# Up products of a routed two-layer network: token parts side by side in half of the groups

## The chip, the cores and the metric

One Trainium2 chip, of which the program uses one core. That core has a matrix engine (TensorE, PE in the tables), whose weights are loaded by instructions of their own (PEld), a vector engine (VectorE, DVE), a scalar engine (ScalarE, ACT), GpSimd (POOL) and a queue engine (SP) that issues most DMAs. The metric is the device time of one execution in microseconds (us), the median over runs; lower is better.

## The reference, cut to what matters

```
state = alpha[:, :, t, :, None] * state + einsum('bhd,bhe->bhde', k[:, :, t], v[:, :, t])   # for every t
y[:, :, t] = einsum('bhd,bhde->bhe', q[:, :, t], state)
...
skip_score = x @ w_skip                      # x: 3072 tokens of 384 numbers
do_compute = skip_score > 0
...
e_idx = argmax(xc @ w_gate, axis=1)          # 8 experts
for e in range(8):
    mask = e_idx == e
    h = maximum(xc[mask] @ w1[e], 0.0)       # 384 -> 1024
    y[mask] = gate_w[mask, None] * (h @ w2[e])   # 1024 -> 384
out[do_compute] = xc + y
```

A linear attention gives 3072 tokens. Those with a positive skip score go to one expert each, and each expert is two matrix products with a ReLU between. All numbers are float32.

## The kernel before, in words

**Two stages.** The first 114 us are the attention and the routing. The rest, which the change touches, is the method `experts`: eight experts one after the other. An expert works on a fixed number of token places, `USED`, from 240 down to 192. Experts 0 and 1 have fixed numbers; experts 2 to 7 are the other six, sorted on the chip by how many tokens they got, so that the fullest comes first.

**Split products.** Each float32 number is split into a high part in TensorE's own format and a remainder (names end in `h` and `l`). A product is the sum of three: high weight by high token, low weight by high token, high weight by low token. The tokens of an expert, turned so that features lie on partitions, stand in `xx[:, k, part, :]`: for each of three blocks k of 128 features first the high part, then, 256 columns on, the low part.

**One expert.** `up(e, g)`, four groups g, each with two column tiles f of 128: 2 x 3 x 3 = 18 matmuls of `USED` columns into one PSUM bank, each with its own 128x128 weight tile (L806). Then ACT writes the ReLU as high part `hh` (L820) and DVE the remainder `hl` (L821), both straight from the bank. `down(e, j)`, twice, for the two blocks of up to 128 tokens: 8 x 3 = 24 matmuls of 384 columns (L832), then DVE scales and adds (`o`, L835), and POOL scatters the rows to the output (L837). Between the two, `turn(e+1)` transposes the next expert's tokens on TensorE, three blocks by two token blocks (L784), and ACT and DVE split them into `xx` (L786, L787).

**Weights and tokens.** SP loads a weight matrix of an expert in four pieces (L658) into one of two raw buffers in turn: w1, w2, w1, w2 and so on. ACT and DVE split each piece (L672, L675). Two w1 pieces are split ahead of each half of `down`, a w2 piece ahead of each `up`. POOL gathers the token rows of an expert by an indirect DMA for each token block (L640) from a list of row numbers. Each engine's instructions stand in the order in which the program issues them.

**The sorted order.** `order_experts` is a chain of 17 small DVE instructions (L727 to L753). Its first eleven end with `by`, a selector with which two small matmuls reorder the row lists of the experts (`order_rows`, L755, into `by_idx`). The other six give `order_ids`, the experts' numbers (`by_order` in the trace), which SP reads into registers (`load_order`, L770); the addresses of the weight loads of experts 2 to 7 come from them. Before the change the whole chain stands in expert 0 behind `turn(1)`, ahead of the second `down`; `order_rows` and the gather for expert 2 stand inside `up(1, 0)`, and the w1 load of expert 2 behind `down(0, 1)`.

**Banks.** The first `up` of all takes bank 0 of `ps_y`; after that `ps_k`, `ps_s[0]` and `ps_s[1]` take turns. `turn` writes both banks of `ps_y`.

Of the kernel before, what the change touches and what calls it, by code (L numbers as in the profile page):

```python
# [17 lines left out]
ALU = mybir.AluOpType  # L18
# [17 lines left out]
CAP = 256  # L36
USED = (240, 240, 240, 228, 216, 208, 200, 192)
FIXED = 2
VW = 3 * E
NB = CAP // P  # L40
SEG = P + 3
# [23 lines left out]
class Kernel:  # L65
# [612 lines left out]
    def expert_pools(self, st):  # L678
        tc = self.tc
        self.mp = st.enter_context(tc.tile_pool(name="mp", bufs=2))  # L680
        self.wpool["w2"] = st.enter_context(tc.tile_pool(name="wp2", bufs=1))
        self.wpool[1] = st.enter_context(tc.tile_pool(name="wp1", bufs=1))
        self.ew = {}
        self.up_bank = 0

    def gather(self, e):
        xr = self.xrb[e % len(self.xrb)]
# [31 lines left out]
    def order_experts(self):  # L719

        nc, const = self.nc, self.const
        t = lambda name, *s, dt=F32: const.tile([P, *s], dt, name="by_" + name)
        count = t("count", E)
        key, ge, pos, at = t("key", E), t("ge", E, E), t("pos", E), t("at", E, E)
        nums = self.slots[:, 0:E]
        v = nc.vector
        v.tensor_copy(count, self.ps_d[:, 320:320 + E])  # L727
        v.scalar_tensor_tensor(out=key, in0=count, scalar=float(E), in1=self.rank, op0=ALU.mult, op1=ALU.add)
        for e in range(FIXED):
            v.memset(key[:, e:e + 1], 2.0 ** (22 - e))  # L730
        v.tensor_tensor(ge, key.unsqueeze(1).to_broadcast([P, E, E]), key.unsqueeze(2).to_broadcast([P, E, E]), ALU.is_ge)
        v.tensor_reduce(out=pos, in_=ge, op=ALU.add, axis=AX.X)
        mine, part, place = t("mine", E), t("part", 3), t("place", 1)
        r = slice(0, VW)
        ec = self.ident[r, r].rearrange("p (e c) -> p e c", c=3)
        v.tensor_reduce(out=mine[r], in_=ec, op=ALU.add, axis=AX.X)
        v.tensor_reduce(out=part[r], in_=ec.rearrange("p e c -> p c e"), op=ALU.add, axis=AX.X)
        v.tensor_tensor(mine[r], mine[r], pos[r], ALU.mult)
        v.tensor_reduce(out=place[r], in_=mine[r], op=ALU.add, axis=AX.X)
        self.by = t("by", E, 3)  # L740
        v.scalar_tensor_tensor(out=self.by[r], in0=nums[r].unsqueeze(2).to_broadcast([VW, E, 3]), scalar=place[r],
                               in1=part[r].unsqueeze(1).to_broadcast([VW, E, 3]), op0=ALU.is_equal, op1=ALU.mult)
        who, ids = t("who", E, E), t("ids", E)
        self.order_ids = t("order", E, dt=I32)
        one = slice(0, 1)
        v.tensor_tensor(at[one], pos[one].unsqueeze(1).to_broadcast([1, E, E]),
                        nums[one].unsqueeze(2).to_broadcast([1, E, E]), ALU.is_equal)
        v.tensor_tensor(who[one], at[one], nums[one].unsqueeze(1).to_broadcast([1, E, E]), ALU.mult)
        v.tensor_reduce(out=ids[one], in_=who[one], op=ALU.add, axis=AX.X)
        v.tensor_scalar(out=self.order_ids[one], in0=ids[one], scalar1=-1.0, scalar2=None, op0=ALU.add)  # L750
        v.tensor_tensor(who[one], at[one], count[one].unsqueeze(1).to_broadcast([1, E, E]), ALU.mult)
        self.counts = t("counts", E)
        v.tensor_reduce(out=self.counts[one], in_=who[one], op=ALU.add, axis=AX.X)  # L753
# [20 lines left out]
    def turn(self, e):  # L774

        nc, w = self.nc, self.ew[e]
        xr = w["xr"]
        w["xx"] = xx = self.mp.tile([P, KT, 2, CAP], F32R, name="xx")
        ps = self.ps_y.rearrange("p b t -> p (b t)")[:, :KT * CAP].rearrange("p (k s) -> p k s", k=KT)
        u = USED[e]  # L780
        for k in range(KT):
            for j in range(NB):
                r = slice(0, min(u - j * P, P))
                nc.tensor.transpose(ps[:, k, j * P:j * P + r.stop], xr[r, j, k * P:(k + 1) * P], self.ident[r, r])  # L784
        for s in (slice(0, 2), slice(2, KT)):
            nc.scalar.copy(out=xx[:, s, 0, :u], in_=ps[:, s, :u])  # L786
            nc.vector.tensor_tensor(xx[:, s, 1, :u], ps[:, s, :u], xx[:, s, 0, :u].bitcast(F32), ALU.subtract)  # L787

    def up(self, e, g):
        nc, w = self.nc, self.ew[e]  # L790
        if g == 0:
            w["hh"], w["hl"] = (self.mp.tile([P, FT, CAP], F32R, name=n) for n in ("hh", "hl"))
        w1h, w1l = (a.rearrange("p (f k c) -> p f k c", k=KT, c=P) for a in self.wt[e]["w1"][:2])
        xx = w["xx"]
        ps = (self.ps_k, *self.ps_s)[self.up_bank % 3] if self.up_bank else self.ps_y[:, 0, :]
        used = USED[e]
        ps = ps.rearrange("p (u s) -> p u s", u=2)[:, :, :used]
        self.up_bank += 1
        terms = (w1h, 0), (w1l, 0), (w1h, 1)
        order = [(u, t, k) for u in range(2) for t in range(3) for k in range(KT)]  # L800
        if e == 0 and g == 0:
            order.sort(key=lambda o: (o[1] == 2, o[2]))
        for n, (u, t, k) in enumerate(order):
            f = 2 * g + u
            a, b = terms[t]
            nc.tensor.matmul(ps[:, u, :], lhsT=a[:, f, k, :], rhs=xx[:, k, b, :used], start=(n == 0),  # L806
                             stop=(n == len(order) - 1))
            if (e, g, n) == (0, 2, 6):
                self.finish_table()
                next(self.second)  # L810
            if (e, g, n) == (0, 2, 14):
                self.finish_rows()
            if (e, g, n) == (0, 3, 8):
                self.count_all()
            if (e, g, n) == (1, 0, 14):
                self.order_rows()
                self.gather(FIXED)
        gs = slice(2 * g, 2 * g + 2)
        hh, hl = w["hh"][:, gs, :used], w["hl"][:, gs, :used]
        nc.scalar.activation(out=hh, in_=ps, func=AF.Relu)  # L820
        nc.vector.scalar_tensor_tensor(out=hl, in0=ps, scalar=0.0, in1=hh.bitcast(F32), op0=ALU.max, op1=ALU.subtract)  # L821
# [219 lines left out]
    @staticmethod  # L1041
    def advance(it, n=1):
        for _ in range(n):
            next(it, None)
# [205 lines left out]
    def experts(self):  # L1250
# [3 lines left out]
        for e in range(E):  # L1254
            second = self.second = self.split_pieces(e, "w2")
            for g in range(FT // 2):
                if (e, g) in ((5, 0), (5, 2)):
                    self.must_redo(g)
                if e > 0:
                    advance(second)  # L1260
                self.up(e, g)
                if (e, g) == (0, 2):
                    advance(second, 2)
            advance(second)
# [6 lines left out]
            self.down(e, 0)  # L1271
            if e + 1 < E:
                self.turn(e + 1)
            if e == 0:
                self.order_experts()
                self.load_order()
            advance(first, 2)
            self.down(e, 1)
            if e + 2 < E:
                advance(self.weight_pieces(e + 2, "w1"), 4)  # L1280


# [48 lines left out]
```

## Time and profile before

| | |
|---|---|
| median of 3 runs | 261.66 us (261.10 to 262.69) |
| profiled execution | 261.22 us, of which 259.4 us span from the first to the last instruction |
| granted TensorE clock, mean | 0.995 |
| busy in the span: PE, DVE, ACT, POOL | 249.7, 198.8, 146.7, 142.5 us |
| matmul instructions | 3394 |

Times in the profile count from the span's first instruction. A row of the timeline merges neighbouring instructions of one kind, so its second number is the time from the first start to the last modelled end; the pace of matmuls is read from one start to a later start. "x6" is the number of instructions in the row. A bracket at the end of a row is idle time of that engine before it and what ended the wait.

### The profile page before, as it was taken

To read this page: it belongs to the slowest core of one execution; us is meant where nothing else is said; L and a number is where in the kernel's file an instruction comes from. 1 tells how busy PE (TensorE), PEld (TensorE's weight loads), DVE (VectorE), ACT (ScalarE), POOL (GpSimd) and SP (SyncE) were. 2 spreads that over 40 slices of the span, in tenths; PEclk is the share of its full clock that TensorE was granted. 3 is DMA by queue.
4 is the path that set the end of the run, shared out by engine and by line. 5 is a ranking of instruction groups with operands and counts; after the bars stand their busy time and mean duration, and the time that the engine had idled before them with its cause. 6 is when DMAs were issued, how large, how long until landed. Compare 5 with 4: busy or idle time off the path is not lost.

```text
span 259.4 us, 8502 instructions
## 1 busy us (share of the span) xinstructions
PE 249.7 (96%) x3394; PEld 230.8 (89%) x3394; DVE 198.8 (77%) x398; ACT 146.7 (57%) x302; POOL 142.5 (55%) x190
## 2 busy tenths in 40 slices
PE   7899999999999999999999999999999999999990
PEld 7688888888989888789999999999999999989980
DVE  5999999889898898577988678676776777756600
ACT  5488555587778795465646446463663544535400
POOL 6899888999896898983618450151321502011011
PEclk9999999999999999999999999999999999999998
DMA  6999999899988954156558966486466755671000
GB/s 229 375 396 377 309 335 302 308 352 348 331 290 286 314 162 157 41 184 243 168 207 304 325 196 212 192 308 236 150 208 266 241 183 165 238 246 41 0 35 12
DMA packets 24462, 60.12 MB, mean 232 GB/s; under 512 B 3678, under 2 KB 9159, under 8 KB 24416
## 3 DMA queue, kind: packets, MB, share of 16 engines
q1 hardware_dynamic: 22016, 54.17, 60.6%
q0 software_dynamic: 2112, 5.08, 5.5%
q8 instruction: 28, 0.46, 0.7%
q10 hardware_dynamic: 288, 0.27, 0.3%
q14 instruction: 18, 0.15, 0.2%
HBM read 52.02 MB, written 8.21 MB: 232 GB/s over the span
## 4 chain that ended last, share of the span: by engine, by line
PE 89%; POOL 3%; DVE 2%; DMA 2%; SPq 0%; issue 0%; ACT 0%; POOLq 0%; DVEq 0%
PE ps_s L806 16%; PE ps_v L832 13%; PE ps_g L832 13%; PE ps_s L279 8%; PE ps_k L806 8%; PE ps_y L342 8%; PE ps_g L375 7%; PE ps_k L300 3%; PE ps_y L322 3%; PE ps_v L334 3%; PE ps_y L784 2%; DMA qkv<-in_tiles_dram 2%; POOL qkv L258 1%; PE ps_v L548 1%; POOL qkv L254 1%; PE ps_y L806 1%
## 5 line engine op out<-in xcount | busy, mean ns | idle before, releaser
L837 POOL DMA_INDIRECT out_dram<-o,by_idx x12 | 12.0, 999 | 77.3 <-DVE o L835 73.5
L806 PE MATMUL ps_s<-xx,w1h 128*128 128x240 f32 (+5 forms) x252 | 37.6, 276 | 0.0
L675 DVE TENSOR_TENSOR w2l<-raw,w2h 128x768 fp32r<-128x768 f32 x32 | 30.7, 961 | 3.4 <-ACT w2h L672 2.0
L806 PEld LDWEIGHTS ps_s<-xx,w1h 128*128 128x128 f32 x252 | 32.9, 191 | 0.2
L258 POOL TENSOR_TENSOR qkv<-qkv,pfx 112x512 f32<-112x512 f32 (+1 forms) x27 | 29.0, 1079 | 6.5 <-DVE pfx L247 5.6
L672 ACT CAST w2h<-raw 128x768 fp32r<-128x768 f32 x32 | 26.4, 829 | 8.7 <-issue 8.7
L234 DVE TENSOR_TENSOR_SCAN sfx<-qkv,ps_d 112x524 f32<-112x524 f32 (+1 forms) x25 | 29.6, 1187 | 1.9 <-DMA qkv<-in_tiles_dram 1.9
L247 DVE TENSOR_TENSOR_SCAN pfx<-qkv,ps_d 112x524 f32<-112x524 f32 (+1 forms) x27 | 29.8, 1113 | 0.8
L254 POOL TENSOR_TENSOR qkv<-qkv,sfx 112x512 f32<-112x512 f32 (+1 forms) x25 | 28.6, 1147 | 3.0 <-DVE sfx L234 2.9
L279 PE MATMUL ps_s<-qkv 48*64 48x128 f32 x768 | 26.7, 276 | 1.7 <-POOL qkv L258 1.6
L675 DVE TENSOR_TENSOR w1l<-raw,w1h 128x768 fp32r<-128x768 f32 x28 | 25.6, 954 | 2.7 <-ACT w1h L672 2.1
L279 PEld LDWEIGHTS ps_s<-qkv 48*64 48x64 f32 x768 | 20.7, 133 | 6.4 <-POOL qkv L258 3.2
L672 ACT CAST w1h<-raw 128x768 fp32r<-128x768 f32 (+1 forms) x36 | 25.8, 762 | 0.0
L342 PE MATMUL ps_y<-st,qkv 128*48 128x128 f32 x368 | 25.6, 274 | 0.0
L832 PE MATMUL ps_v<-w2h,hh 128*112 128x384 f32 (+5 forms) x64 | 21.9, 343 | 0.0
L820 ACT ACTIVATE hh<-ps_s 128x480 fp32r<-128x480 f32 (+5 forms) x21 | 11.3, 539 | 18.7 <-PE ps_s L806 17.9
L832 PE MATMUL ps_v<-w2h,hl 128*112 128x384 f32 (+5 forms) x64 | 21.5, 336 | 0.0
L832 PE MATMUL ps_g<-w2h,hh 128*128 128x384 f32 x64 | 21.5, 336 | 0.0
L832 PE MATMUL ps_v<-w2l,hh 128*112 128x384 f32 (+5 forms) x64 | 21.5, 336 | 0.0
L832 PE MATMUL ps_g<-w2h,hl 128*128 128x384 f32 x64 | 21.5, 335 | 0.0
L832 PE MATMUL ps_g<-w2l,hh 128*128 128x384 f32 x64 | 21.4, 335 | 0.0
L806 PE MATMUL ps_s<-xx,w1l 128*128 128x240 f32 (+5 forms) x126 | 20.9, 275 | 0.0
(230 smaller groups left out, 598.1 us busy)
## 6 DMA issues: line engine op xcount, KB each, us to landing
raw<-in_w_dram SPq DMA_DIRECT2D x62, 384.0 KB, 3.3
qkv<-in_tiles_dram SPq DMA_DIRECT2D x18, 518.0 KB, 6.5
qkv<-in_tiles_dram SPq DMA_DIRECT2D x18, 448.0 KB, 7.1
out_dram<-x SPq DMA_DIRECT2D x24, 192.0 KB, 3.1
qkv<-in_tiles_dram SPq DMA_DIRECT2D x4, 512.0 KB, 6.5
qkv<-in_tiles_dram SPq DMA_DIRECT2D x5, 262.0 KB
qkv<-in_tiles_dram SPq DMA_DIRECT2D x6, 192.0 KB
qkv<-in_tiles_dram SPq DMA_DIRECT2D x3, 256.0 KB, 4.9
```

The source lines that it names most:

```text
L234: nc.vector.tensor_tensor_scan(sfx[:PD, a:a + n][:, ::-1], w["alpha"][:PD, a:a + n][:, ::-1], self.c_r[:PD].to_broadcast([PD, n]), LOW, AL ...
L247: nc.vector.tensor_tensor_scan(pfx[:PD, a:a + n], w["alpha"][:PD, a:a + n], self.c_f[:PD].to_broadcast([PD, n]), 0.0, ALU.mult, ALU.max)
L254: (eng or self.nc.gpsimd).tensor_tensor(w["kh"][:PD, s], w["kh"][:PD, s], w["sfx"][:PD, s, 3:SEG], ALU.mult)
L258: (eng or nc.gpsimd).tensor_tensor(w["qh"][:PD, s], w["qh"][:PD, s], w["pfx"][:PD, s, 2:2 + P], ALU.mult)
L279: nc.tensor.matmul(self.ps_s[h][s, p * P:(p + 1) * P], lhsT=kh[r, p, s], rhs=qh[r, p, :], start=True, stop=True)
L342: nc.tensor.matmul(self.y_out(i, p, h), lhsT=w["v"][:, o:o + D], rhs=w["st"][:, h, p * P:(p + 1) * P], start=(i < B and p < 2), stop=(p >= 2))
L375: nc.tensor.matmul(pg[s, p, :], lhsT=w["xt"][:PD, p, s], rhs=self.xw[:PD, p, :], start=True, stop=True)
L672: nc.scalar.copy(out=hi[:, s], in_=raw[:, s])
L675: (nc.gpsimd if step < STEP else nc.vector).tensor_tensor(lo[:, s], raw[:, s], hi[:, s].bitcast(F32), ALU.subtract)
L806: nc.tensor.matmul(ps[:, u, :], lhsT=a[:, f, k, :], rhs=xx[:, k, b, :used], start=(n == 0), stop=(n == len(order) - 1))
L832: nc.tensor.matmul(ps, lhsT=a[:, f, js], rhs=b[:, f, :], start=(n == 0), stop=(n == 3 * FT - 1))
L837: ins = nc.gpsimd.indirect_dma_start(out=self.out[:, :], out_offset=bass.IndirectOffsetOnAxis(ap=self.slots_of(e)[r, j:j + 1], axis=0), in ...
```

## The change

From expert 2 on, groups 0 and 2 of the up products are made by a new method, `up_pairs`. For each column tile f it uses a bank of its own: three matmuls of the high weight stream both token parts side by side (2 x `USED` columns, both halves of the bank), then three of the low weight stream the high part into the second half, on top of high weight by low part. ACT copies the second half to an SBUF tile `h`, DVE adds the first half to it, and ReLU and remainder are then made from `h`, issued behind the matmuls of the next group. The banks `ps_y[:, 0]`, `ps_s[0]`, `ps_s[1]` and `ps_k` take turns in all groups; a paired group takes two.

Three more edits: the second token block of an expert is transposed with at least 72 rows, which changes the last expert alone (64 before); the two halves of `order_experts` move behind `down(0, 1)` and behind `up(1, 0)`, with `load_order` and the w1 load of expert 2 behind the second half; `order_rows` moves into `up(1, 2)` and the gather for expert 2 behind it.

```diff
@@ -36,6 +36,7 @@
 CAP = 256
 USED = (240, 240, 240, 228, 216, 208, 200, 192)
 FIXED = 2
+PAIRED = ((), (), (0, 2), (0, 2), (0, 2), (0, 2), (0, 2), (0, 2))
 VW = 3 * E
 NB = CAP // P
 SEG = P + 3
@@ -681,7 +682,7 @@
         self.wpool["w2"] = st.enter_context(tc.tile_pool(name="wp2", bufs=1))
         self.wpool[1] = st.enter_context(tc.tile_pool(name="wp1", bufs=1))
         self.ew = {}
-        self.up_bank = 0
+        self.relus, self.up_bank = [], 0
 
     def gather(self, e):
         xr = self.xrb[e % len(self.xrb)]
@@ -740,6 +741,7 @@
         self.by = t("by", E, 3)
         v.scalar_tensor_tensor(out=self.by[r], in0=nums[r].unsqueeze(2).to_broadcast([VW, E, 3]), scalar=place[r],
                                in1=part[r].unsqueeze(1).to_broadcast([VW, E, 3]), op0=ALU.is_equal, op1=ALU.mult)
+        yield
         who, ids = t("who", E, E), t("ids", E)
         self.order_ids = t("order", E, dt=I32)
         one = slice(0, 1)
@@ -780,11 +782,47 @@
         u = USED[e]
         for k in range(KT):
             for j in range(NB):
-                r = slice(0, min(u - j * P, P))
+                r = slice(0, min(max(u - j * P, 72), P))
                 nc.tensor.transpose(ps[:, k, j * P:j * P + r.stop], xr[r, j, k * P:(k + 1) * P], self.ident[r, r])
         for s in (slice(0, 2), slice(2, KT)):
             nc.scalar.copy(out=xx[:, s, 0, :u], in_=ps[:, s, :u])
             nc.vector.tensor_tensor(xx[:, s, 1, :u], ps[:, s, :u], xx[:, s, 0, :u].bitcast(F32), ALU.subtract)
+
+    def up_pairs(self, e, g):
+
+        nc, w, used = self.nc, self.ew[e], USED[e]
+        if g == 0:
+            w["hh"], w["hl"] = (self.mp.tile([P, FT, CAP], F32R, name=n) for n in ("hh", "hl"))
+        w1h, w1l = (a.rearrange("p (f k c) -> p f k c", k=KT, c=P) for a in self.wt[e]["w1"][:2])
+        xx = w["xx"]
+        banks = [self.next_bank(), self.next_bank()]
+        h = self.mp.tile([P, 2, CAP], F32, name="h")[:, :, :used]
+        sums = []
+        for u in range(2):
+            f = 2 * g + u
+            ps = banks[u][:, :2 * used].rearrange("p (t s) -> p t s", t=2)
+            for k in range(KT):
+                nc.tensor.matmul(ps, lhsT=w1h[:, f, k, :], rhs=xx[:, k, :, :used], start=(k == 0), stop=False)
+            for k in range(KT):
+                nc.tensor.matmul(ps[:, 1, :], lhsT=w1l[:, f, k, :], rhs=xx[:, k, 0, :used], start=False,
+                                 stop=(k == KT - 1))
+            sums.append(ps)
+        self.flush(self.relus)
+        for u, ps in enumerate(sums):
+            nc.scalar.copy(out=h[:, u, :], in_=ps[:, 1, :])
+            nc.vector.tensor_tensor(h[:, u, :], ps[:, 0, :], h[:, u, :], ALU.add)
+
+        def relu():
+            hh, hl = (w[n][:, 2 * g:2 * g + 2, :used] for n in ("hh", "hl"))
+            nc.scalar.activation(out=hh, in_=h, func=AF.Relu)
+            nc.vector.scalar_tensor_tensor(out=hl, in0=h, scalar=0.0, in1=hh.bitcast(F32), op0=ALU.max,
+                                           op1=ALU.subtract)
+        self.relus.append(relu)
+
+    def next_bank(self):
+
+        self.up_bank += 1
+        return (self.ps_y[:, 0, :], *self.ps_s, self.ps_k)[(self.up_bank - 1) % 4]
 
     def up(self, e, g):
         nc, w = self.nc, self.ew[e]
@@ -792,10 +830,9 @@
             w["hh"], w["hl"] = (self.mp.tile([P, FT, CAP], F32R, name=n) for n in ("hh", "hl"))
         w1h, w1l = (a.rearrange("p (f k c) -> p f k c", k=KT, c=P) for a in self.wt[e]["w1"][:2])
         xx = w["xx"]
-        ps = (self.ps_k, *self.ps_s)[self.up_bank % 3] if self.up_bank else self.ps_y[:, 0, :]
+        ps = self.next_bank()
         used = USED[e]
         ps = ps.rearrange("p (u s) -> p u s", u=2)[:, :, :used]
-        self.up_bank += 1
         terms = (w1h, 0), (w1l, 0), (w1h, 1)
         order = [(u, t, k) for u in range(2) for t in range(3) for k in range(KT)]
         if e == 0 and g == 0:
@@ -810,11 +847,11 @@
                 next(self.second)
             if (e, g, n) == (0, 2, 14):
                 self.finish_rows()
+            if (e, g, n) == (1, 2, 14):
+                self.order_rows()
             if (e, g, n) == (0, 3, 8):
                 self.count_all()
-            if (e, g, n) == (1, 0, 14):
-                self.order_rows()
-                self.gather(FIXED)
+        self.flush(self.relus)
         gs = slice(2 * g, 2 * g + 2)
         hh, hl = w["hh"][:, gs, :used], w["hl"][:, gs, :used]
         nc.scalar.activation(out=hh, in_=ps, func=AF.Relu)
@@ -1258,7 +1295,13 @@
                     self.must_redo(g)
                 if e > 0:
                     advance(second)
-                self.up(e, g)
+                (self.up_pairs if g in PAIRED[e] else self.up)(e, g)
+                if (e, g) == (1, 0):
+                    advance(order)
+                    self.load_order()
+                    advance(self.weight_pieces(FIXED, "w1"), 4)
+                if (e, g) == (1, 2):
+                    self.gather(FIXED)
                 if (e, g) == (0, 2):
                     advance(second, 2)
             advance(second)
@@ -1271,12 +1314,12 @@
             self.down(e, 0)
             if e + 1 < E:
                 self.turn(e + 1)
-            if e == 0:
-                self.order_experts()
-                self.load_order()
             advance(first, 2)
             self.down(e, 1)
-            if e + 2 < E:
+            if e == 0:
+                order = self.order_experts()
+                next(order)
+            if 0 < e < E - 2:
                 advance(self.weight_pieces(e + 2, "w1"), 4)
 
 
```

How this moves instructions, at two places. First DVE in expert 1. Before: the end of the chain, then split pieces, the second result `o` of expert 0, and the row lists `by_idx` ahead of the first `hl` of expert 1:

```order
L750 TENSOR_SCALAR by_order<-by_ids 1x8
L751 TENSOR_TENSOR by_who<-by_at,by_count 1x64
L753 TENSOR_REDUCE by_counts<-by_who 1x8
L675 TENSOR_TENSOR w1l<-raw,w1h 128x768 x2
L835 SCALAR_TENSOR_TENSOR o<-ps_v,gates,xr_67 112x384
L675 TENSOR_TENSOR w2l<-raw,w2h 128x768
L568 TENSOR_SCALAR by_idxn<-ps_d 128x12
L569 SCALAR_TENSOR_TENSOR by_idx<-ps_d,by_idxn 128x2x6
L709 TENSOR_REDUCE by_gates<-ps_d 128x12
L821 SCALAR_TENSOR_TENSOR hl<-ps_s_76,hh 128x2x240
```

In the changed kernel the chain begins only behind the last two w1 pieces and the second `o` of expert 0:

```order
L789 TENSOR_TENSOR xx<-ps_y,xx 128x240
L676 TENSOR_TENSOR w1l<-raw,w1h 128x768 x2
L872 SCALAR_TENSOR_TENSOR o<-ps_v,gates,xr_67 112x384
L728 COPY by_count<-ps_d 128x8
L729 SCALAR_TENSOR_TENSOR by_key<-by_count,rank 128x8
```

And its end, the row lists, and what stands among them there:

```order
L752 TENSOR_SCALAR by_order<-by_ids 1x8
L753 TENSOR_TENSOR by_who<-by_at,by_count 1x64
L755 TENSOR_REDUCE by_counts<-by_who 1x8
L676 TENSOR_TENSOR w2l<-raw,w2h 128x768
L858 SCALAR_TENSOR_TENSOR hl<-ps_s_76,hh 128x2x240
L676 TENSOR_TENSOR w2l<-raw,w2h 128x768
L569 TENSOR_SCALAR by_idxn<-ps_d 128x12
L570 SCALAR_TENSOR_TENSOR by_idx<-ps_d,by_idxn 128x2x6
L710 TENSOR_REDUCE by_gates<-ps_d 128x12
L858 SCALAR_TENSOR_TENSOR hl<-ps_s_77,hh 128x2x240
```

What moved: two more `w2l` pieces and two `hl` now stand ahead of `by_idx`, one pair of them within the chain itself, between its eleventh and twelfth instruction.

Second, TensorE in the first group of expert 2. Before (18 matmuls of 240 columns into one bank):

```order
L806 MATMUL ps_s_77<-xx,w1h 128x240 x3
L806 MATMUL ps_s_77<-xx,w1l 128x240 x3
L806 MATMUL ps_s_77<-xx,w1h 128x240 x6
L806 MATMUL ps_s_77<-xx,w1l 128x240 x3
L806 MATMUL ps_s_77<-xx,w1h 128x240 x3
```

In the changed kernel (12 matmuls into two banks, then the next group's first three):

```order
L805 MATMUL ps_y<-xx,w1h 128x480 x3
L807 MATMUL ps_y<-xx,w1l 128x240 x3
L805 MATMUL ps_s_76<-xx,w1h 128x480 x3
L807 MATMUL ps_s_76<-xx,w1l 128x240 x3
L843 MATMUL ps_s_77<-xx,w1h 128x240 x3
```

What moved: of nine matmuls for a column tile three are gone, and three stream 480 columns in place of 240.

## Rows read from the trace of the kernel before

**Rows 1.** Page, busy time (share) by engine, and granted clock in 40 slices.
```profile
PE 249.7 (96%) x3394; PEld 230.8 (89%) x3394; DVE 198.8 (77%) x398; ACT 146.7 (57%) x302; POOL 142.5 (55%) x190
...
PEclk9999999999999999999999999999999999999998
```

**Rows 2.** Timeline of PE, expert 2 (start us, us, engine, line, op, out<-in, count).
```profile
150.62 0.50 PE L806 MATMUL ps_s<-xx,w1h 128*128 128x240 f32 x3
...
158.69 0.34 PE L832 MATMUL ps_g<-w2h,hh 128*128 128x384 f32 x1
...
162.86 0.76 PE L784 MATMUL ps_y<-ident,xr 128*128 128x128 f32 x6
```

**Rows 3.** Timeline of PE, expert 7: first up matmul, first down matmul.
```profile
236.53 0.48 PE L806 MATMUL ps_s<-xx,w1h 128*128 128x192 f32 x3
...
244.55 0.36 PE L832 MATMUL ps_g<-w2h,hh 128*128 128x384 f32 x1
```

**Rows 4.** Timeline of PE, matmuls of 256 columns at the attention's end.
```profile
113.79 0.28 PE L613 MATMUL ps_s<-hot,latel 128*128 128x256 f32 x1
...
114.03 0.28 PE L613 MATMUL ps_v<-hot,latel 128*128 128x256 f32 x1
```

**Rows 5.** Timeline of PE, transposes for experts 6 and 7, and what follows them.
```profile
214.06 0.69 PE L784 MATMUL ps_y<-ident,xr 128*128 128x128 f32 x6
214.55 0.38 PE L832 MATMUL ps_v<-w2h,hh 128*80 128x384 f32 x1
...
230.97 1.40 PE L784 MATMUL ps_y<-ident,xr 128*128 128x128 f32 x6
232.31 0.40 PE L832 MATMUL ps_v<-w2h,hh 128*72 128x384 f32 x1
```

**Rows 6.** Timeline of ACT, a 128x240 copy out of PSUM.
```profile
147.94 0.36 ACT L786 CAST xx<-ps_y 128x240 fp32r<-128x240 f32 x1 [0.72 <-issue]
```

**Rows 7.** Timeline of DVE, end of expert 0 and first two groups of expert 1.
```profile
130.53 0.41 DVE L787 TENSOR_TENSOR xx<-ps_y,xx 128x240 fp32r<-128x240 f32 x1 [0.42 <-ACT xx L786]
130.86 0.16 DVE L727 COPY by_count<-ps_d 128x8 f32<-128x8 f32 x1
...
132.50 0.20 DVE L746 TENSOR_TENSOR by_at<-by_pos,slots 1x64 f32<-1x64 f32 x1
...
133.68 1.81 DVE L675 TENSOR_TENSOR w1l<-raw,w1h 128x768 fp32r<-128x768 f32 x2
135.42 0.60 DVE L835 SCALAR_TENSOR_TENSOR o<-ps_v,gates,xr 112x384 f32<-112x384 f32 x1
135.95 0.94 DVE L675 TENSOR_TENSOR w2l<-raw,w2h 128x768 fp32r<-128x768 f32 x1
136.81 0.15 DVE L568 TENSOR_SCALAR by_idxn<-ps_d 128x12 f32<-128x12 f32 x1
...
137.17 0.65 DVE L821 SCALAR_TENSOR_TENSOR hl<-ps_s,hh 128x480 fp32r<-128x480 f32 x1
137.74 0.95 DVE L675 TENSOR_TENSOR w2l<-raw,w2h 128x768 fp32r<-128x768 f32 x1
```

**Rows 8.** Timeline of PE: expert 1's first up matmul, expert 2's transposes.
```profile
132.82 0.50 PE L806 MATMUL ps_s<-xx,w1h 128*128 128x240 f32 x3
...
145.83 0.79 PE L784 MATMUL ps_y<-ident,xr 128*128 128x128 f32 x6
```

**Rows 9.** Timeline of POOL, the two gathers for expert 2.
```profile
138.05 1.57 POOL L640 DMA_INDIRECT xr<-out_dram,by_idx  x1 [0.30 <-DVE hl L821]
139.93 1.09 POOL L640 DMA_INDIRECT xr<-out_dram,by_idx  x1 [0.31 <-issue]
```

**Rows 10.** Timeline of SP, first weight load of expert 2 (and 15 behind it).
```profile
135.84 25.26 SPq L658 DMA_DIRECT2D raw<-in_w_dram  x16
```

**Rows 11.** All gathers (L640), issue to landing.
```profile
DMA to landing us min/median/max: 3.2/5.8/6.7
```

**Rows 12.** Busy us by stretch: PE, PEld, DVE, ACT, POOL, granted clock, DMA, GB/s.
```profile
254.50:256.00 1.50, 0.00 (x0) 0.00 (x0) 0.00 (x0) 0.00 (x0) 0.41 (x1) 1.00 0.18 40
```

## Prediction

> **What bounds the kernel now.** I read the page first. TensorE is busy for 96% of the span, at a granted clock of nine tenths or more in every slice but the last [rows 1]; VectorE has 77%, ScalarE 57%. A busy TensorE need not be at its best pace, so I then read the pace from starts in the timeline. In expert 2, 72 up matmuls of 240 columns take 158.69 - 150.62 = 8.07 us, 112.1 ns each; the 24 matmuls of 384 columns behind them take 162.86 - 158.69 = 4.17 us, 173.8 ns each [rows 2]. In expert 7 the up matmuls have only 192 columns, and take 244.55 - 236.53 = 8.02 us, 111.4 ns each [rows 3]. So an up matmul costs 112 ns whatever its width: something that each pays once sets the pace, by the look of it the 128x128 weight load (PEld is busy for 89% [rows 1]), while wider matmuls are paid by columns: 256 columns take 0.24/2 = 120 ns [rows 4], and (173.8 - 120)/128 = 0.42 ns is the price of a column. There is time to take out of up, by fewer and wider matmuls, as long as everything that TensorE waits for stays early. Where it is not early, TensorE's wait adds in full.
>
> **What is removed and added on TensorE.** For a column tile, nine matmuls of 112 ns go, and three wide ones and three narrow ones come. On the line of 0.42 ns a column through 120 ns at 256, widths 480, 456, 432, 416, 400 and 384 (experts 2 to 7) cost 214, 204, 194, 187, 180 and 174 ns. The saving for a tile is 6 x 111.75 - 3 x width price: 28, 58, 89, 109, 129, 149 ns, together 0.56 us; with four such tiles in each expert, **2.25 us**. No row shows a matmul of over 384 columns here. If price goes in proportion from 384 (480 at 217 ns), the saving is 2.1 us; if the wide ones cost 0.42 ns a column and nothing beside, 3.2 us. I take 2.25, since two widths lie on that line.
>
> The last expert's transposes: with 64 rows the six of them hold TensorE from 230.97 to 232.31, 1.34 us; for expert 6, with 72 rows, from 214.06 to 214.55, 0.49 us [rows 5]. The change gives expert 7 the shape of expert 6, so **0.85 us** goes. Bounds: nothing, if the excess were the place and not the shape; 0.85 since nothing else differs. TensorE's sum is 3.1 us.
>
> **What is added on ScalarE and VectorE.** 24 copies of about 0.36 us [rows 6] and 24 adds of about 0.41 us [rows 7], four of each in an expert. VectorE's load while an expert's up products run: four `w2l` pieces at 0.86 (135.95 to 136.81), four `hl` at 0.57 (137.17 to 137.74), one `o` at 0.53 (135.42 to 135.95), and now four adds: 3.4 + 2.3 + 0.5 + 1.6 = 7.8 us in about 7.8 us of TensorE [rows 7]. It becomes nearly full there. But the last group's `hl` is wanted only from the 19th matmul of `down` on, 18 x 0.174 = 3.1 us later [rows 2], and `down` gives VectorE room. ScalarE has more. The wide group's bank is wanted again at least a group (2 us) later. Cost taken: nothing; the cover is these 3.1 us, and a rival below says what it costs if it is gone.
>
> **What is moved.** This is the term that decides. I rebuild VectorE's queue in expert 1 from the starts of the rows before. The second `o` of expert 0 can't start before `down(0, 1)` ends, about 133.0 [rows 8], and VectorE is free by then (its two w1 pieces, 1.74 us from 133.68 to 135.42 before, follow `xx`, which ends at 130.94 [rows 7]). Behind it stand, in the new order: `o` 0.53, the first part of the chain 1.64 (130.86 to 132.50), a `w2l` 0.86, an `hl` 0.57, the second part 1.18 (132.50 to 133.68), `w2l` 0.86, `hl` 0.57, `w2l` 0.86 [rows 7]. That puts the row lists' first instruction at 133.0 + 7.07 = 140.1 and `by_idx` at 140.4. Before, the first was at 136.81: 3.3 us later.
>
> Two things hang on it. First, SP: the second part starts at 136.6 in place of 132.50, and the first weight load of expert 2 was issued at 135.84, 3.34 us after it [rows 10]. Now 139.9, four microseconds later. Those weights are wanted by splits that lead `up(2, 0)` at 150.62 [rows 2], so I cost this at nothing; but those four loads, and the w2 loads that no longer have a gap before them, now stand in the DMA queues just when the gather comes.
>
> Second, POOL: the first gather for expert 2 starts at 140.4 + 0.3 = 140.7 in place of 138.05, the second 1.88 us later (as 139.93 to 138.05 [rows 9]), at 142.6. A gather takes 3.2 us to land at the least, 5.8 in the median, 6.7 at the most [rows 11]. TensorE wants both blocks at 145.83 [rows 8]; nothing earlier in expert 1 makes TensorE faster or slower. Landing at 145.8, 148.4 or 149.3 gives a wait of 0, 2.6 or 3.5 us. Before, the second gather had landed 5.9 us after its issue at the latest, since the transposes did not wait for it. I take 5.5 us, a little under the median, since the loads are now denser: landing at 148.1, **2.3 us** of wait. The transposes lead everything that follows, so all of it is lost. The clock is not: in 254.5 to 256, with TensorE idle since about 253, it is still granted in full [rows 12].
>
> **Sum.** 261.22 - 2.25 - 0.85 + 2.3 = 260.4 us against the profiled execution, which lies 0.44 under the median of the runs; against that median it is 260.9. I say **260.6 us**: a small gain, of which the late gather eats three quarters.
>
> **Rivals.** All times against the profiled execution; 1% (2.6 us) is about what a measurement of this kernel can tell from no change.
> - The gather lands in time. For it: the shortest landing is 3.2 us, which just does. Against it: that is the minimum, and the loads of expert 2 now overlap it wholly. The time would be 261.2 - 3.1 = 258.1. Chance 0.21. The Trainium skill (DMA: Bandwidth & Descriptors, section on the anatomy of a GpSimd DMA, its paragraph on arbitration) says that each DMA engine takes turns between its queues packet by packet, by which a gather on its own queue would not stand behind all of the weight loads and would land near the short end, for this 258.1; the trace speaks for it less than against it, with 5.8 us in the median.
> - VectorE becomes the bound in up (the other sign). The add must wait for the copy, which stands behind a ScalarE split; with 0.5 to 0.7 us of such waits for each of four halves, VectorE's 7.8 us become 10 to 10.6. It decides from 7.8 + 3.1 = 10.9 us on. If it goes 0.8 us beyond in six experts: 260.4 + 4.8 = 265.2. Against it: the two halves of a group come a microsecond apart, so that a copy is mostly done when VectorE gets to its add. Chance 0.06.
> - The change doesn't give what it says: a wide matmul costs two narrow ones, 224 ns, so that three of them and three narrow ones cost the same 1008 ns as nine. Then only the transposes gain: 261.2 - 0.85 + 2.3 = 262.7. Against it: 384 columns cost 174. Chance 0.06.
>
> **Chances and range.** My forecast has 0.67; its own range is 259.3 (wait 1.2) to 261.8 (wait 3.5 and a saving of 2.1, against the profiled run 261.8). The 80% range takes in the gather in time and a little of the third: 258.3 to 262.2. Faster by over 1% means under 259.0: the first rival but for its late part, 0.19. Slower by over 1% means over 264.3: the second rival, 0.05. The rest, 0.76, is within 1%.
>
> **What would show it.** Up groups 0 and 2 of expert 2 at about 1.95 us, of expert 7 at 1.71, against 2.01; 72 fewer matmuls; expert 7's transposes at 0.49 us; `by_idxn` at about 140.1; a TensorE wait for the gather's landing ahead of expert 2's transposes, near 2.3 us; no waits of TensorE on VectorE from expert 2 on. I am wrong if that wait is under 1 us or over 4, or if TensorE waits in other places.

## The result and the profile after

The changed kernel takes **264.43 us** (median of 4 runs, 264.24 to 265.64), the kernel before 261.63 us beside it; the ratio is 1.0116, with a 95% interval of 1.0085 to 1.0146. It is slower by about 3 us, outside the range of the forecast. The profiled execution took 264.53 us, of which 262.7 us are span.

The page of the changed kernel, busy time by engine and granted clock in 40 slices:

```profile
PE 249.3 (95%) x3322; PEld 229.7 (87%) x3322; DVE 204.4 (78%) x422; ACT 153.9 (59%) x326; POOL 139.2 (53%) x190
...
PEclk9999999999999999999999779999999999999998
```

Against [rows 1], 72 matmuls are gone, but TensorE is busy for only 0.4 us less, and two slices of the clock have fallen. The timeline of PE shows what happened there (columns as in [rows 2]; a bracket is idle time and its releaser):

```profile
127.54 0.79 PE L786 MATMUL ps_y<-ident,xr 128*128 128x128 f32 x6
...
145.14 0.34 PE L869 MATMUL ps_g<-w2h,hl 128*128 128x384 f32 x1
148.45 0.48 PE L786 MATMUL ps_y<-ident,xr 128*128 128x128 f32 x1 [2.98 <-DMA xr<-out_dram,by_idx]
150.09 1.25 PE L786 MATMUL ps_y<-ident,xr 112*128 112x112 f32 x5 [1.16 <-DMA xr<-out_dram,by_idx]
151.02 0.64 PE L869 MATMUL ps_v<-w2h,hh 128*112 128x384 f32 x1
151.46 0.52 PE L869 MATMUL ps_v<-w2l,hh 128*112 128x384 f32 x1
151.78 0.52 PE L869 MATMUL ps_v<-w2h,hl 128*112 128x384 f32 x1
...
156.89 0.82 PE L805 MATMUL ps_y<-xx,w1h 128*128 128x480 f32 x3
157.55 0.50 PE L807 MATMUL ps_y<-xx,w1l 128*128 128x240 f32 x3
...
164.89 0.34 PE L869 MATMUL ps_g<-w2h,hh 128*128 128x384 f32 x1
...
240.43 0.70 PE L805 MATMUL ps_s<-xx,w1h 128*128 128x384 f32 x3
...
247.87 0.36 PE L869 MATMUL ps_g<-w2h,hh 128*128 128x384 f32 x1
```

TensorE waits for both gathers of expert 2, and behind the waits the down matmuls start 0.32 us apart (151.46 to 151.78) instead of 0.17. The same stretch, busy us by engine, granted clock, DMA share and GB/s, one microsecond to a row:

```profile
147.00:148.00 1.00, 0.00 (x0) 0.00 (x0) 0.07 (x1) 0.00 (x0) 0.64 (x1) 0.89 0.98 379
...
149.00:150.00 1.00, 0.00 (x0) 0.00 (x0) 0.00 (x0) 0.00 (x0) 0.00 (x0) 0.50 1.01 336
...
153.00:154.00 1.00, 1.00 (x4) 0.95 (x4) 0.63 (x2) 1.00 (x3) 0.00 (x0) 0.50 0.56 210
...
155.00:156.00 1.00, 1.00 (x7) 1.00 (x6) 0.61 (x1) 0.00 (x0) 0.00 (x0) 1.00 0.02 6
```

While TensorE stands idle the granted clock goes from 1.00 to 0.50 (2.4 to 1.2 GHz), and in this execution it is back at 1.00 only after TensorE has worked for some four microseconds behind the second wait. The DMA engines are full (0.98, 1.01) all through the wait. What was issued just before, on POOL and on SP, and the one landing that the profile tells of the four gathers issued here, that of the third (expert 3's first, issued at 143.82):

```profile
141.13 1.06 POOL L641 DMA_INDIRECT xr<-out_dram,by_idx  x1 [5.84 <-DVE by_gates L710]
142.49 1.02 POOL L641 DMA_INDIRECT xr<-out_dram,by_idx  x1 [0.30 <-issue]
...
140.34 4.79 SPq L659 DMA_DIRECT2D raw<-in_w_dram  x8
...
DMA to landing us min/median/max: 7.6/7.6/7.6
```

The landings of expert 2's own gathers are read from TensorE's waits: the first was there by 148.45, at most 7.3 us after its issue, the second by 150.09, 150.09 - 142.49 = 7.6 us. Both weight matrices of expert 2, eight loads, are issued within 4.8 us around the two gathers. Before, they were two groups, the first from 135.84 on [rows 10].

**The loss and the gain by stage.** The transposes of expert 1 in the kernel before:

```profile
128.03 0.79 PE L784 MATMUL ps_y<-ident,xr 128*128 128x128 f32 x6
```

From there to the transposes of expert 2 it is 17.80 us before the change (128.03 to 145.83 [rows 8]), so here they were due at 127.54 + 17.80 = 145.34. With the 4.79 us that lie between transposes and first up product before (145.83 to 150.62 [rows 2]), 22.59 us in all, that product was due at 150.13. It starts at 156.89, **6.76 us late**. From there to expert 7's first down product the changed kernel needs 247.87 - 156.89 = 90.98 us against 244.55 - 150.62 = 93.93 [rows 2, 3], **2.95 us less**. The first stage was 0.49 us shorter in this execution. 261.22 + 6.76 - 2.95 - 0.49 = 264.54, and 264.53 was measured: the account is closed, and only the 6.76 us need explaining.

### The profile page after: what moved, and what is told of

Same layout as the page of the kernel before. It is cut to its first block, busy times and chain, and to the rows that moved or that the text cites. A ratio compares the mean times of both kernels' runs of the same rounds, so it can differ in the third digit from the quotient of the medians.

```text
span 262.7 us, 8404 instructions
## 1 busy us (share of the span) xinstructions
PE 249.3 (95%) x3322; PEld 229.7 (87%) x3322; DVE 204.4 (78%) x422; ACT 153.9 (59%) x326; POOL 139.2 (53%) x190
## 4 chain that ended last, share of the span: by engine, by line
PE 75%; DMA 10%; DVE 5%; POOL 4%; issue 3%; SPq 1%; POOLq 0%; ACT 0%; DVEq 0%
PE ps_v L869 12%; PE ps_g L869 10%; PE ps_s L280 8%; PE ps_y L343 7%; PE ps_g L376 7%; PE ps_s L843 5%; DMA xr<-out_dram,idx 4%; PE ps_k L301 3%; PE ps_y L323 3%; DMA xr<-out_dram,by_idx 3%; PE ps_s L805 3%; PE ps_v L335 3%; PE ps_y L843 2%; PE ps_k L843 2%; DMA qkv<-in_tiles_dram 2%
## 5 line engine op out<-in xcount | busy, mean ns | idle before, releaser
L869 PE MATMUL ps_v<-w2h,hh 128*112 128x384 f32 (+5 forms) x64 | 22.7, 355 | 0.0
L869 PE MATMUL ps_v<-w2l,hh 128*112 128x384 f32 (+5 forms) x64 | 22.2, 346 | 0.0
L869 PE MATMUL ps_v<-w2h,hl 128*112 128x384 f32 (+5 forms) x64 | 22.1, 345 | 0.0
L788 ACT CAST xx<-ps_y 128x480 fp32r<-128x480 f32 (+11 forms) x14 | 6.0, 432 | 26.1 <-PE ps_y L786 21.4
L286 ACT COPY st<-ps_s 128x512 f32<-128x512 f32 x26 | 15.1, 583 | 10.3 <-PE ps_s L280 10.3
L376 PE MATMUL ps_g<-xw,xt 112*64 112x105 f32 x352 | 20.9, 259 | 0.0
L343 PEld LDWEIGHTS ps_y<-st,qkv 128*48 128x48 f32 x368 | 20.4, 123 | 0.2
```

The lines of the kernel that those rows point to most:

```text
L286: self.nc.scalar.copy(out=w["st"][:, h, :], in_=self.ps_s[h])
L343: nc.tensor.matmul(self.y_out(i, p, h), lhsT=w["v"][:, o:o + D], rhs=w["st"][:, h, p * P:(p + 1) * P], start=(i < B and p < 2), stop=(p >= 2))
L376: nc.tensor.matmul(pg[s, p, :], lhsT=w["xt"][:PD, p, s], rhs=self.xw[:PD, p, :], start=True, stop=True)
L869: nc.tensor.matmul(ps, lhsT=a[:, f, js], rhs=b[:, f, :], start=(n == 0), stop=(n == 3 * FT - 1))
```

## The experiments

Theory 1: the row lists, and with them the gather's issue, come too late, and the rest follows. Theory 2: it is not the issue alone; the loads that the move crowds around the gather stretch its landing. Theory 3: the pairs or the turning banks cost the time.

**Every move undone** (pairs, banks and 72 rows stay).

```diff
-        yield                                   # in order_experts
...
-            if (e, g, n) == (1, 2, 14):
-                self.order_rows()
...
+            if (e, g, n) == (1, 0, 14):
+                self.order_rows()
+                self.gather(FIXED)
...
+            if e == 0:                          # behind turn(1)
+                self.order_experts()
+                self.load_order()
...
+            if e + 2 < E:                       # behind down(e, 1)
                 advance(self.weight_pieces(e + 2, "w1"), 4)
```

> The changed kernel with every move undone: the chain that orders the experts, the row lists, both gathers of expert 2 and its first weight loads stand where they stood before the change. Pairs, four banks and 72 rows stay. Late gather (theory 1) and crowded transfers (theory 2) both expect no wait of TensorE ahead of expert 2, a granted clock of 1.00 all through, and 258.1 to 258.6 us (261.6 less 2.25 for the wide matmuls and 0.85 for the 72 rows), a ratio near 0.988 to the kernel before. If the pairs or the turning banks themselves cost the time (theory 3), it stays at 262 us or more.

Measured: 258.79 us, ratio 0.9894 (0.9853 to 0.9936). Its PE timeline, from the transposes of expert 2 on:

```profile
145.20 0.79 PE L785 MATMUL ps_y<-ident,xr 128*128 128x128 f32 x6
...
150.00 0.81 PE L804 MATMUL ps_y<-xx,w1h 128*128 128x480 f32 x3
...
240.96 0.36 PE L869 MATMUL ps_g<-w2h,hh 128*128 128x384 f32 x1
```

No wait, and 90.96 us from the second row to the third, as in the changed kernel. Theory 3 is out: the whole loss comes with the moves.

**The moves alone**, on the kernel before.

> The kernel before with the moves alone, without pairs, four banks or 72 rows. Theories 1 and 2: TensorE waits 4 to 5 us for the gather ahead of expert 2's transposes, the granted clock falls behind it, and the time is 6 to 7 us above the kernel before, 267.5 to 268.5 us. Theory 3 (the pairs cost the time): about 261.6 us, no change.

Measured: 267.3 us, ratio 1.0234 (1.0180 to 1.0289), 6.1 us by the ratio (4.7 to 7.6). Its wait of TensorE (us in total, times, longest):

```profile
PE ps_y L785 <- DMA xr<-out_dram,by_idx: 3.6, 2, 2.6
```

**First weights early, row lists and gathers late.** The chain is whole again behind `turn(1)`, with `load_order`; the w1 load goes back behind `down(0, 1)`.

```diff
-        yield                                   # in order_experts
...
-                if (e, g) == (1, 0):
-                    advance(order)
-                    self.load_order()
-                    advance(self.weight_pieces(FIXED, "w1"), 4)
...
```

> The changed kernel with the chain, the expert order and expert 2's first weight loads back in their old place (loads issued near 136 us), while the row lists and both gathers of expert 2 stay late (issued near 141 and 142.5 us). Theory 1 (the issue time decides, landing takes over 7 us whatever else is under way): TensorE still waits 4 to 5 us and the time is 263.5 to 264.5 us. Theory 2 (the two weight matrices of expert 2 crowd the gathers): they land 4.3 to 5.8 us after issue as before the change, TensorE waits 0.5 to 2 us, and the time is 259 to 260.5 us.

Measured: 260.63 us, ratio 0.996 (0.9926 to 0.9994). The two gathers, issued at 140.07 and 141.44, from issue to landing, and TensorE's one wait in the timeline and in the stretch of 149 to 150 us:

```profile
DMA to landing us min/median/max: 3.9/5.1/6.4
...
145.58 0.27 PE L785 MATMUL ps_y<-ident,xr 128*128 128x128 f32 x1
147.86 0.74 PE L785 MATMUL ps_y<-ident,xr 112*128 112x112 f32 x5 [2.01 <-DMA xr<-out_dram,by_idx]
...
149.00:150.00 1.00, 1.00 (x5) 0.95 (x4) 0.66 (x1) 0.28 (x2) 0.00 (x0) 0.50 0.67 222
```

Over half of the loss is gone, as theory 2 had it, though wait and time lie at the upper end of what it expected. Both theories have a share: against the changed kernel the second gather is issued 1.05 us earlier (141.44 against 142.49) and lands 1.2 us sooner after its issue (6.4 against 7.6). The granted clock falls here too, behind a single wait of 2 us.

**Gathers early, weights late.** The first half of the chain goes back behind `turn(1)`, `order_rows` and the gather into `up(1, 0)`; its second half, `load_order` and the w1 load stay behind `up(1, 0)`.

> The changed kernel with the row lists and both gathers of expert 2 back in the first group of expert 1 (issued near 138 and 140 us), while the chain's second half, the expert order and expert 2's first weight loads stay late (issued from about 140 us). Theory 1: no wait for the gather and, if the weights land in time, 258.1 to 258.8 us. Theory 2: the gathers are still crowded by the weights, and the second lands 7 us after its issue, near 147 us, which makes TensorE wait 1 to 2 us, 259.5 to 260.5 us. If expert 2's first weights, landing near 150 us, are what it waits for next, TensorE waits up to 3 us at the first up product instead.

Measured: 258.83 us, ratio 0.9902 (0.9874 to 0.9930). The gathers, issued at 136.49 and 137.86, ahead of the loads (from 139.96):

```profile
DMA to landing us min/median/max: 3.1/3.5/3.8
```

No wait of TensorE. Weights that come 4 us later cost nothing themselves. Theory 2's wait did not come: both gathers were issued ahead of the crowd, and the second, which landed 1.7 us after the first load was issued, took 3.8 us.

**The second matrix behind the transposes**, on the kernel with the late row lists: the loads of expert 2's w2 stand behind `turn(2)` in the program.

> The kernel of the late row lists (first weights of expert 2 early, row lists and gathers late), with the loads of expert 2's second weight matrix held back until the transposes of expert 2 are issued, so that no weight load is issued near the two gathers. Theory 2 (crowding): the second gather lands 4 to 5 us after its issue instead of 6.4, TensorE's wait ahead of expert 2 falls from 2.3 us to 1 us or less, unless the late second matrix is waited for in its place. Theory 1 (a landing time of its own): the second gather still lands 6 us or more after its issue and TensorE waits 2 us.

Measured: 260.23 us, ratio 0.9963 (0.9927 to 1.0000). The edit missed its aim: SP did not wait for TensorE, and in the profiled execution, the longest of ten at 263.78 us, the loads were still issued from 143.52 on, half a microsecond behind the second gather. That one's landing and TensorE's wait:

```profile
DMA to landing us min/median/max: 6.3/6.3/6.3
...
PE ps_y L785 <- DMA xr<-out_dram,by_idx: 1.9, 1, 1.9
```

It tells nothing between the theories, so the loads were then held by data.

**The second matrix held by the gather's data**, on the kernel with the late row lists.

```diff
+        if (e, name) == (FIXED, "w2"):          # in weight_pieces, ahead of the loads
+            r = slice(0, USED[e] - P)
+            self.nc.gpsimd.tensor_copy(raw[r, 0:1], self.ew[e]["xr"][r, 1, 0:1])
```

> The kernel of the late row lists (first weights of expert 2 early, row lists and gathers late), with the loads of expert 2's second weight matrix made to wait until the second gather of expert 2 has landed (GpSimd copies one column of its rows into the matrix's buffer first; the load overwrites it). GpSimd then also issues expert 3's gathers later. Theory 2 (crowding): the second gather lands 4 to 5 us after its issue instead of 6.4, near 146 us, and TensorE waits under 1 us ahead of expert 2, though the late matrix may be waited for behind that. Theory 1 (a landing time of its own): it still lands over 6 us after its issue.

Measured: 257.82 us, ratio 0.9882 (0.9846 to 0.9919). POOL's timeline, the landing of the first gather, and the stretch of 144 to 150 us:

```profile
140.00 1.06 POOL L641 DMA_INDIRECT xr<-out_dram,by_idx  x1 [2.56 <-DVE by_gates L713]
141.37 1.31 POOL L641 DMA_INDIRECT xr<-out_dram,by_idx  x1 [0.31 <-issue]
144.78 0.18 POOL L655 COPY raw<-xr 112x1 f32<-112x1 f32 x1 [2.10 <-DVE w1l L679]
...
DMA to landing us min/median/max: 3.1/3.1/3.1
...
144.00:150.00 6.00, 6.00 (x39) 5.95 (x38) 3.63 (x6) 2.39 (x4) 3.34 (x4) 1.00 0.68 222
```

The copy, which needs the second gather, was released at 144.78 by a VectorE split and not by the gather, which had thus landed within 3.4 us of its issue. The issue times are those of the kernel with the late lists (140.07 and 141.44); the transfers issued behind the gathers are gone, and with them wait, clock loss and the whole cost. **Theory 2 holds for these issue times**: gathers issued 1.4 to 2 us later than before the change cost nothing when the transfers behind them are held, and 2 us of wait and the clock when they are not. Two things stay open. The copy also holds back expert 3's two gathers (of 0.2 MB; from 143.07 to 145.53), so the run does not tell them apart from the four weight loads (of 0.4 MB). And the changed kernel issues 1.1 us later still: with a landing of 3.4 us its second gather would come at 145.9, some 0.6 us after it is wanted. That is an estimate; no run has it.

**The clock by itself.** 24, then 40 independent matmuls ahead of the waiting transposes keep TensorE busy; their sums are not used.

```diff
...
+            if e == 1:                          # behind down(1, 0)
+                self.fill(FILL)                 # 240 columns each, into ps_v
             if e + 1 < E:
                 self.turn(e + 1)
```

> The changed kernel with 24 independent matmuls of 240 columns (about 0.11 us each, 2.6 us together, their sums unused) ahead of the transposes that wait for the gather of expert 2, so that TensorE is busy through most of the first wait. The gather itself is as late as in the changed kernel. If the fall of the granted clock behind the wait costs time of its own, the clock stays higher in the stretch of 150 to 156 us and the time falls by 1.5 to 2 us against the changed kernel, to 262.3 to 263 us (with the whole 24 matmuls inside the wait). If the clock costs nothing (as the prediction had it), the time stays at 264 to 264.5 us.

> The changed kernel with 40 independent matmuls (some 4.4 us, their sums unused) ahead of the transposes of expert 2, so that TensorE is busy through nearly the whole wait for the gather, which is as late as before. If the fall of the granted clock costs time of its own: granted clock 1.00 all through, 4.2 us from the first down product behind the transposes to expert 2's first up product instead of 5.9, and 1 to 1.7 us less than the changed kernel in the same call. If not: the same time as the changed kernel.

> The changed kernel itself once more, on the same chip as the other three of this call, so that small differences can be told: 264.2 to 264.6 us, and the wait of 4 to 5 us ahead of expert 2 in its profile.

Measured: 24 matmuls 264.2 us, ratio 1.0105 (1.0060 to 1.0151); 40 matmuls 263.86 us, ratio 1.0135 (1.0090 to 1.0180), and beside the latter the changed kernel again 264.87 us, ratio 1.0144 (1.0119 to 1.0170). With 40 matmuls:

```profile
127.44 0.79 PE L787 MATMUL ps_y<-ident,xr 128*128 128x128 f32 x6
...
149.69 1.13 PE L787 MATMUL ps_y<-ident,xr 128*128 128x128 f32 x6
150.59 0.41 PE L877 MATMUL ps_v<-w2h,hh 128*112 128x384 f32 x1
...
154.81 0.82 PE L806 MATMUL ps_y<-xx,w1h 128*128 128x480 f32 x3
...
144.00:150.00 6.00, 5.96 (x49) 5.74 (x48) 2.45 (x3) 1.22 (x2) 3.04 (x3) 1.00 1.00 352
150.00:156.00 6.00, 5.92 (x36) 5.81 (x37) 3.50 (x6) 3.23 (x6) 0.09 (x1) 1.00 0.55 192
```

The clock stays at 1.00, and the second half of `down` takes 154.81 - 150.59 = 4.22 us, where the changed kernel needs 156.89 - 151.02 = 5.87. So 1.65 us of the loss in that execution are clock. By the whole stage it is 2.0: from expert 1's transposes to expert 2's first up product it takes 154.81 - 127.44 = 27.37 us, 4.78 more than the 22.59 before the change, where the changed kernel has 6.76. This assumes that the second gather landed equally late in both, as it roughly did: behind the 40 matmuls the profile still has PEld wait 0.3 us for it. In the medians 1.0 us of it shows (264.87 to 263.86), in the ratios 0.2, with intervals that overlap: the stage shows the clock term, the total does not settle its size, since the gather's landing changes from run to run.

With 24 matmuls the median missed the 262.3 to 263 us that were expected if the clock costs. The profiled execution (263.12 us) shows the clock kept, though TensorE waits behind them for a second gather that took 8.1 us to land:

```profile
150.77 0.74 PE L787 MATMUL ps_y<-ident,xr 112*128 112x112 f32 x5 [2.36 <-DMA xr<-out_dram,by_idx]
...
150.00:156.00 6.00, 5.23 (x32) 5.16 (x33) 3.12 (x5) 2.64 (x5) 0.00 (x0) 1.00 0.66 220
```

Its stage takes 155.51 - 127.43 = 28.08 us, 5.5 more than before the change and 1.3 less than in the changed kernel.

**The two gains by themselves**: 72 rows alone, and pairs with four banks alone, on the kernel before.

> The kernel before with the second half of a transpose taking at least 72 rows, nothing else of the change. The prediction's term: only expert 7 had 64 rows there; its transposes take 0.49 us instead of 1.34, so 0.85 us less, 260.7 us, a ratio of 0.9967. If the slow transposes were hidden beside something else: 261.5 us, no change.

> The kernel before with the pairs and the four banks alone, without the moves and without the 72 rows. The prediction's term: 2.25 us less (bounds 2.1 to 3.2), 259.3 us, a ratio of 0.991. If the copies and adds on ScalarE and VectorE hold TensorE up: 261.5 us or more.

Measured: 72 rows 260.03 us, ratio 0.9951 (0.9922 to 0.9981); pairs 259.76 us, ratio 0.9912 (0.9880 to 0.9944). The stage tells more closely. First up product of expert 2, with 72 rows alone, then with pairs alone, each followed by expert 7's first down product:

```profile
149.89 0.50 PE L806 MATMUL ps_s<-xx,w1h 128*128 128x240 f32 x3
...
242.95 0.36 PE L832 MATMUL ps_g<-w2h,hh 128*128 128x384 f32 x1
```

```profile
152.19 0.81 PE L804 MATMUL ps_y<-xx,w1h 128*128 128x480 f32 x3
...
244.02 0.36 PE L869 MATMUL ps_g<-w2h,hh 128*128 128x384 f32 x1
```

93.06 and 91.83 us against 93.93: **0.87 us** from the 72 rows, **2.10 us** from the pairs.

**All four groups side by side**, moves undone: the best version.

```diff
-PAIRED = ((), (), (0, 2), (0, 2), (0, 2), (0, 2), (0, 2), (0, 2))
+PAIRED = ((), ()) + 6 * (tuple(range(4)),)
...
+            self.flush(self.relus)              # behind the four groups of an expert
             advance(second)
```

> The kernel with every move undone, and all four groups of up products from expert 2 on side by side instead of the first and third. If the saving per group holds: another 2.25 us less than with two groups a stage, 256.5 us. If VectorE and ScalarE, which get two more copies and two more adds of 0.36 us for each such group, become late for TensorE's banks: 258.8 us or more.

Measured: **256.45 us**, ratio 0.9818 (0.9789 to 0.9848). Page and stage:

```profile
PE 246.1 (96%) x3250; PEld 226.0 (88%) x3250; DVE 210.7 (82%) x446; ACT 160.2 (63%) x350; POOL 141.4 (55%) x190
```

```profile
151.99 0.81 PE L804 MATMUL ps_y<-xx,w1h 128*128 128x480 f32 x3
...
240.82 0.36 PE L869 MATMUL ps_g<-w2h,hh 128*128 128x384 f32 x1
```

88.83 us, another 2.13 under the version with two paired groups (90.96); VectorE at 82% holds nothing up yet. It beats the kernel before by 4.7 us by the ratio, and the changed kernel by 8.

## Why the prediction was wrong, step by step

- **Wide matmuls**: 2.25 us forecast, 2.10 measured. Three matmuls of 480 columns take 157.55 - 156.89 = 0.66 us, 220 ns each; the line through 256 and 384 columns gave 214, the bound in proportion 217. The saving lies on the lower bound that was named. The rival in which a wide one costs two narrow ones (224 ns) nearly holds at 480 columns: expert 2's up products take 164.89 - 156.89 = 8.00 us against 8.07 [rows 2]. It is out further on, where `USED` is smaller: expert 7's take 247.87 - 240.43 = 7.44 us against 8.02 [rows 3].
- **72 rows**: 0.85 forecast, 0.87 measured.
- **Copies and adds at nothing**: right. The profile lists no wait of TensorE for VectorE or ScalarE in expert 2 and later ones, and twice as many of them still cost nothing.
- **Moved order, the lists**: `by_idxn` was forecast at 140.1 and the gathers at 140.7 and 142.6. VectorE's timeline:

```profile
133.40 0.62 DVE L872 SCALAR_TENSOR_TENSOR o<-ps_v,gates,xr 112x384 f32<-112x384 f32 x1 [0.80 <-DMA xr<-out_dram,idx]
...
140.49 0.15 DVE L569 TENSOR_SCALAR by_idxn<-ps_d 128x12 f32<-128x12 f32 x1
```

  The rebuilt queue was right to 0.4 us. What it lacked is in the first row: `o` of expert 0 waits for its own rows, a wait that the rebuilt queue did not have. The gathers came at 141.13 and 142.49.
- **Moved order, the landing. This is the step that failed.** "I take 5.5 us, a little under the median, since the loads are now denser: landing at 148.1". The second gather landed 7.6 us after its issue, above the 6.7 us that I used as the upper bound [rows 11]; with the same order it took 6.8 us in the run of the moves alone and 8.1 with 24 matmuls. I had named the crowd in the same paragraph, and then took less than the median for it, where denser loads speak for more. The spread of 3.2 to 6.7 us was no spread of chance: with the first matrix issued 4 us ahead the landings are 3.9 and 6.4 us, with the second held too 3.1 and at most 3.4. The trace of before had this in it. Its longest landing is that of expert 0's second gather:

```profile
126.69 1.50 POOL L640 DMA_INDIRECT xr<-out_dram,idx  x1 [0.30 <-issue]
...
DMA to landing us min/median/max: 6.7/6.7/6.7
```

  Four weight loads were issued around it, from 126.48 to 128.3, and the gather issued at 125.35, ahead of them, landed after 3.3 us. So 6.7 us was the price beside four loads, and the change brought eight. The wait forecast at 2.3 us, at most 3.5, became 2.98 + 1.16 = 4.14 us of idle time, over the 4 us that the prediction named as its sign of being wrong.
- **"The clock is not [lost]". This failed too.** I read it from a stretch at the program's end where the clock was still granted in full [rows 12]. Two rows further on, the same view of before shows it fallen, with TensorE still idle:

```profile
257.00:258.00 1.00, 0.00 (x0) 0.00 (x0) 0.00 (x0) 0.00 (x0) 0.00 (x0) 0.53 0.03 8
```

  So that stretch could not stand for every wait, and no work of TensorE came behind it to show a cost. Here the clock fell during the wait and cost 1.65 us in `down`, and with the transposes about 2.0. In the kernel with the late lists the second gather landed at 147.8, almost where I had forecast it, and the clock fell there as well. So even with the right landing, the term for the wait was short.
- **Together**: 6.76 us late instead of 2.3 is 4.46 more than forecast. With 0.15 less saved and a first stage that was 0.49 shorter in that execution, 260.42 + 4.46 + 0.15 - 0.49 = 264.54, against 264.53 measured.
- **The rival with the gather in time** fell here, but for a reason that can be undone: with the loads held, the very gathers land in 3.1 and at most 3.4 us. The rule of the Trainium skill that stood beside it (DMA: Bandwidth & Descriptors, section on queues, rings and completion order, its paragraph on arbitration) did not foretell the landing in the changed kernel: whatever turns the queues take, 7.6 us beside eight weight loads and 3.1 to 3.4 with the second four held back is what these runs show. **VectorE as the bound** did not come about. (Its terms add up to 9.8 to 10.6 us, not 10 to 10.6.)

## What to carry to other kernels

When a move delays the source of an address or index, list everything that hangs on it, and see what will be in the DMA queues at the new time: a transfer's price has to be read from one with the same neighbours, not from the spread of all. A wait ahead of a busy matrix engine can cost more than its length, since the work behind it may start at the lower clock. And a good change can come together with a bad one: tried apart, the pairs gained 2.1 us, and twice as many gained as much again.

## What the runs showed of the hardware that was not expected

- A gather of 128 rows of 1.5 KB landed 3.1 us after its issue with no weight load issued around it (the first one of the run with early gathers). One of 112 rows took 6.4 us with four loads issued behind it (late lists), and 6.8 to 8.1 us with eight around it (moves alone, changed kernel, 24 matmuls).
- The granted clock fell to 0.50 in a wait of 2.98 us and behind one of 2.01 us, and stayed there for some four microseconds of work. In the kernel with 24 filling matmuls TensorE waited 2.4 us, and the clock stayed at 1.00; at the end of the kernel before, TensorE was idle from about 253 on, and the clock was at 1.00 up to 257 and at 0.53 behind. The length of the wait alone does not tell.
- The first stage, the same in all these kernels but for the banks of the first up products, does not take the same time in all executions: the transposes of expert 1 began between 127.2 us (moves alone) and 129.6 us (pairs alone). That is as much as the pairs gain; differences of that size are read from a stage's first to its last row, not from the total of one execution.
